# Attention summaries of a fused attention and two-MLP kernel: k, v and phi as head pairs on 128 partitions, in smaller loads

## The chip, the cores and the metric

The kernel runs on one core of a Trainium2 chip. The metric is the device time of one execution in microseconds (us); of three runs the median counts.

## The reference, cut to what matters

There are 8 batches of 8 heads, 576 tokens of 64 numbers, and 32 memory slots. For each head, `phi` is turned into weights over the tokens, which condense k and v to 32 summary rows; the queries then attend to these rows. The result (4608 x 512) goes through two MLPs of width 2048.

```python
a = np.exp(phi - np.max(phi, axis=2, keepdims=True))      # over the tokens
a = a / (np.sum(a, axis=2, keepdims=True) + 1e-09)
k_m = np.einsum('bhsm,bhsd->bhmd', a, k)
v_m = np.einsum('bhsm,bhsd->bhmd', a, v)
scores = scale * np.matmul(q, k_m.transpose(0, 1, 3, 2))
attn = softmax(scores)                                     # over the 32 rows
x = np.matmul(attn, v_m)                                   # heads side by side: 4608 x 512
h = x @ w_in;  x = (h * sigmoid(1.702 * h)) @ w_out        # first MLP
h = x @ w_in2; x = (h * sigmoid(h)) @ w_out2               # second MLP
```

The four weight matrices arrive as 64-bit floats; all else is 32-bit.

## The kernel before, in words

The program has four stages. The first does attention and the first product of the first MLP; the other three do the remaining products with seven block products in place of eight, through intermediate tensors in DRAM (`gs`, `xs`). The change touches only the first stage.

**The slots.** The first stage is a list of 256 slots, 32 to a batch: slot 32*b + 2*f + hf makes 128 of the 2048 columns (f) for one half of the batch's tokens (hf, 288 tokens). `first1` (L314) issues six matmuls of 288 columns on PE (TensorE), a tanh on ACT (ScalarE, L327) and a product on DVE (VectorE, L328) that writes tile `g`. After both halves of an f, `g_store` (L330) stores the 288 KB of `g` to `gs`. There are five `g` buffers and four PSUM buffers for `h`, so PE can run up to four slots ahead of ACT, and ACT at slot 2*(f+5) needs the store of tile f to have landed.

**What a slot multiplies.** The moving operand is `attnT` (the attention weights of a half, `soft_t` to `soft3`, L260 to L298, written as a high and a low part). The stationary one is `slab`: the v summaries times 512 columns of w_in (`wp_mm`, `wp_hi`, `wp_lo`, L300 to L310). A slab (b, c) covers 8 slots. `scores` and `wp_mm` share one PSUM buffer, `aa`, so each waits until the other's reader has emptied it.

**The summaries of a batch.** `load_phi` and `load_kv` (L119, L124) bring 0.59 MB of phi and 2.36 MB of k and v on 96 partitions, six tokens each: one transfer for phi, and k and v each in two transfers of four heads (576 KB). One `kv` buffer holds four heads, so the second group of heads is loaded only after the matmuls of the first. For batches 0 and 1 the second group goes into spare weight buffers, in eight transfers (L130). Then: the maximum over tokens (`fold`, five DVE operations, or one reduction for batch 0, L152), a transpose, a reduction and a broadcast by PE (L157 to L175), subtraction and exponential in two halves (L180, L185), the sum on POOL (GpSimd), 48 matmuls of 96 rows x 32 x 128 columns that give the summaries (`kv_mm`, L189), the division (`kv_norm`, L208), four transposes and a copy (`kvT`).

**w_in.** It comes in 16 pieces of 128 x 512 (four column groups j of four), each converted by two ACT operations (L93, L94), two of DVE (L101, L102) and one of POOL (L104).

**What sets the order.** Each engine executes its own list in order. `at(slot, kind, function)` puts a step into a slot; `plan_attention` (L730) gives the slots for batches 1 to 7 by a table; the code from L800 does so for batch 0, whose steps stand at slots -20 to 0, and for w_in. Up to slot 24 a scheduler reorders what was recorded; from there on the recorded order is final. All transfers are issued by SP (SyncE) on one queue, in order; a transfer whose buffer isn't free yet holds back those behind it.

Of the kernel before, what the change touches and what calls it, by code (L numbers as in the profile page):

```python
# [8 lines left out]
F32 = mybir.dt.float32  # L9
# [12 lines left out]
def attn_moe_moe(ctx: ExitStack, tc: tile.TileContext, q, k, v, phi, w1i, w1o, w2i, w2o, out):  # L22
# [28 lines left out]
    ones = const.tile([128, 1], F32)  # L51
# [67 lines left out]
    def load_phi(b):  # L119
        t = att.tile([P, H, C6, M], F32, tag="phi", name="phi")  # L120
        nc.sync.dma_start(out=t, in_=phi[b].rearrange("h (p c) m -> p h c m", c=C6))
        st["phi", b] = t

    def load_kv(b, g):  # L124
        t = att.tile([P, 2, 4, C6, D], F32, tag="kv", name="kv")
        for i, src in enumerate((k, v)):
            nc.sync.dma_start(out=t[:, i], in_=src[b, 4 * g:4 * g + 4].rearrange("h (p c) d -> p h c d", c=C6))
        st["kv", b, g] = [t[:, :, j] for j in range(4)]

    def load_kv_early(b, rooms):  # L130
# [15 lines left out]
    def fold(b, name, op, eng):  # L146
        x = st["phi", b]
        t = st[name, b] = att.tile([P, H, M], F32, tag=name, name=name)
        for c in range(1, C6):
            eng.tensor_tensor(out=t, in0=t if c > 1 else x[:, :, 0], in1=x[:, :, c], op=op)  # L150

    def phi_fold0(name, op):  # L152
        st[name, 0] = att.tile([P, H, M], F32, tag=name, name=name)
        nc.vector.tensor_reduce(out=st[name, 0], in_=st["phi", 0].rearrange("p h c m -> p h m c"),
                                axis=AX.X, op=op)

    def phi_max_t(b):  # L157
        pm = st.pop(("pm", b)).rearrange("p h m -> p (h m)")
        a = st["a", b] = psa()
        for g in range(2):  # L160
            nc.tensor.transpose(a[:, g * P:(g + 1) * P], pm[:, g * 128:(g + 1) * 128], ident[:P, :P])

    def phi_max_r(b):
        nm = att.tile([128, 2], F32, tag="nm", name="nm")
        nc.vector.tensor_reduce(out=nm, in_=st.pop(("a", b))[:, 0:2 * P].rearrange("p (g s) -> p g s", g=2),
# [3 lines left out]
    def phi_max_b(b):  # L169
        nm = st.pop(("nm", b))  # L170
        a = st["a", b] = psa()
        for g in range(2):
# [906 lines left out]
```

## Time and profile before

| | us |
|---|---|
| median of three runs | 1552.33 (1549.19 to 1562.49) |
| the profiled execution | 1554.82, its span 1553.0 |
| slot 0 starts; from slot 1 on PE runs on | at 42.62; at 57.76 |
| end of the first stage (last of 256 slots) | 424.75 |
| the other three stages | 424.75 to 1553.0 |

The profile gives for each engine when it was busy, and for each idle stretch what ended it (`<-`). The clock is TensorE's granted clock, 1.00 for 2.4 GHz and 0.50 for 1.2 GHz. DMA share is the mean busy share of the 16 transfer engines. A matmul of 32-bit floats appears as two instructions on PE, one in the reduced format `fp32r` (those of L322) as one.

### The profile page before, as it was taken

To read this page: it belongs to the slowest core of one execution; us is meant where nothing else is said; L and a number is where in the kernel's file an instruction comes from. 1 tells how busy PE (TensorE), PEld (TensorE's weight loads), DVE (VectorE), ACT (ScalarE), POOL (GpSimd) and SP (SyncE) were. 2 spreads that over 40 slices of the span, in tenths; PEclk is the share of its full clock that TensorE was granted. 3 is DMA by queue.
4 is the path that set the end of the run, shared out by engine and by line. 5 is a ranking of instruction groups with operands and counts; after the bars stand their busy time and mean duration, and the time that the engine had idled before them with its cause. 6 is when DMAs were issued, how large, how long until landed. Compare 5 with 4: busy or idle time off the path is not lost. (4 is left out here: it accounts for less than half of the span.)

```text
span 1553.0 us, 27494 instructions
## 1 busy us (share of the span) xinstructions
PE 1446.3 (93%) x10432; PEld 1355.6 (87%) x10432; DVE 1158.2 (75%) x1742; ACT 797.8 (51%) x1415; POOL 206.3 (13%) x175
## 2 busy tenths in 40 slices
PE   4789889989879999999989999999998999999998
PEld 2567677778779999999878999999997999999998
DVE  5767666676668878887787877877788777767765
ACT  4545455656534554544545656656565444444443
POOL 2422445441200101010000010110000000000000
PEclk7689899999999999999999999999998999999999
DMA  8677778664737366365334455555456425325230
GB/s 236 195 210 219 203 211 231 219 200 167 248 133 241 98 217 221 102 224 191 104 99 150 153 189 202 165 191 186 169 177 226 144 71 194 112 103 193 86 129 31
DMA packets 202085, 265.54 MB, mean 171 GB/s; under 512 B 51168, under 2 KB 173024, under 8 KB 201952
## 3 DMA queue, kind: packets, MB, share of 16 engines
q1 hardware_dynamic: 201952, 263.77, 52.6%
q8 instruction: 82, 1.34, 0.4%
q14 instruction: 51, 0.42, 0.1%
HBM read 159.91 MB, written 102.76 MB: 169 GB/s over the span
## 5 line engine op out<-in xcount | busy, mean ns | idle before, releaser
L517 PE MATMUL p<-op,wq 128*128 128x384 f32 x2016 | 365.8, 340 | 21.8 <-DVE op L64 12.8
L517 PEld LDWEIGHTS p<-op,wq 128*128 128x128 f32 x2016 | 352.5, 189 | 34.9 <-DVE op L64 23.4
L677 PE MATMUL p<-wq,op 128*128 128x256 f32 x3024 | 360.6, 282 | 4.1 <-DVE gq L619 3.5
L677 PEld LDWEIGHTS p<-wq,op 128*128 128x128 f32 x3024 | 360.2, 191 | 4.8 <-DVE gq L619 4.0
L500 ACT CAST op<-rr 128x768 fp32r<-128x768 f32 x216 | 178.2, 834 | 182.5 <-PE p L677 78.3
L64 DVE TENSOR_TENSOR op<-rr,op 128x768 fp32r<-128x768 f32 x216 | 209.9, 975 | 82.0 <-ACT op L500 79.4
L322 PEld LDWEIGHTS h<-attnT,slab 128*128 128x128 f32 x1536 | 225.2, 203 | 50.9 <-DVE g L328 25.3
L322 PE MATMUL h<-attnT,slab 128*128 128x288 f32 x1536 | 254.2, 318 | 11.6 <-DVE g L328 10.4
L605 PE MATMUL xb<-xq,wq 128*128 128x384 f32 x1152 | 221.5, 341 | 10.8 <-ACT e L637 4.8
L605 PEld LDWEIGHTS xb<-xq,wq 128*128 128x128 f32 x1152 | 202.8, 190 | 16.2 <-ACT e L637 6.0
L328 DVE SCALAR_TENSOR_TENSOR g<-g,h 128x288 f32<-128x288 f32 x256 | 110.2, 444 | 98.9 <-ACT g L327 98.1
L605 PE MATMUL y<-xq,wq 128*128 128x384 f32 x864 | 167.7, 338 | 1.4 <-ACT e L665 0.8
L64 DVE TENSOR_TENSOR op<-r,op 128x768 fp32r<-128x768 f32 x120 | 116.7, 975 | 61.1 <-ACT op L500 60.9
L327 ACT ACTIVATE g<-h 128x288 f32<-128x288 f32 x256 | 103.0, 415 | 106.4 <-PE h L322 66.7
L500 ACT CAST op<-r 128x768 fp32r<-128x768 f32 x120 | 99.7, 834 | 110.8 <-PE p L517 48.7
L605 PEld LDWEIGHTS y<-xq,wq 128*128 128x128 f32 x864 | 152.6, 189 | 2.5 <-ACT e L665 1.5
L614 ACT ACTIVATE gq<-e 128x384 f32<-128x384 f32 x144 | 75.6, 525 | 105.3 <-DVE e L61 102.6
L619 DVE SCALAR_TENSOR_TENSOR gq<-gq,e 128x384 f32<-128x384 f32 x144 | 93.8, 657 | 27.3 <-ACT gq L614 24.6
L104 POOL TENSOR_TENSOR wst<-wst 128x512 int32<-128x512 int32 x24 | 34.1, 1420 | 503.1 <-DVE wst L102 242.7
L428 ACT CAST wq<-wst 128x512 fp32r<-128x512 f32 x83 | 51.2, 618 | 49.4 <-DVE wst L64 24.8
L61 DVE TENSOR_TENSOR e<-e,y 128x384 f32<-128x384 f32 x96 | 52.3, 550 | 17.9 <-PE y L605 15.0
L247 PE MATMUL aa<-w,kvT 64*32 64x512 f32 x512 | 41.1, 673 | 19.7 <-DVE nat L264 15.8
(115 smaller groups left out, 1354.2 us busy)
## 6 DMA issues: line engine op xcount, KB each, us to landing
rr<-gs SPq DMA_DIRECT2D x120, 384.0 KB, 6.2
gs<-g SPq DMA_DIRECT2D x128, 288.0 KB, 4.0
gs<-gq SPq DMA_DIRECT2D x192, 192.0 KB, 2.0
r<-gs SPq DMA_DIRECT2D x72, 384.0 KB, 5.5
xs<-o SPq DMA_DIRECT2D x24, 384.0 KB, 4.4
xr<-xs SPq DMA_DIRECT2D x24, 384.0 KB, 4.5
out_dram<-o SPq DMA_DIRECT2D x24, 384.0 KB, 2.8
q<-in_q_dram SPq DMA_DIRECT2D x124, 72.0 KB, 3.7
```

The costliest lines, as they stand in the source:

```text
L61: eng.tensor_tensor(out=out, in0=a, in1=b, op=ALU.add)
L64: eng.tensor_tensor(out=out, in0=a, in1=b, op=ALU.subtract)
L322: nc.tensor.matmul(out=h, lhsT=slab[b, f // 4, g][:, wi, f0:f0 + 128], rhs=x[:, g, xi], start=(g == 0 and n == 0), stop=(g == 1 and n == 2))
L327: nc.scalar.activation(out=t, in_=h, func=ACTF.Tanh, scale=0.851)
L328: nc.vector.scalar_tensor_tensor(out=t, in0=t, scalar=1.0, in1=h, op0=ALU.add, op1=ALU.mult)
L428: nc.scalar.copy(out=t[:, :, 0], in_=wst[m, c, k])
L500: nc.scalar.copy(out=t[:, :, 0], in_=s)
L517: nc.tensor.matmul(out=out[:, d, :HB], lhsT=w[:, s, wi, d * 128:(d + 1) * 128], rhs=t[:, s, gi], start=(start and p == 0 and s == 0 and n ...
L605: nc.tensor.matmul(out=out, lhsT=w[:, s, wi, f0:f0 + 128], rhs=x[:, s, xi], start=(start and s == 0 and n == 0), stop=(s == 1 and n == 2), ...
L614: nc.scalar.activation(out=t, in_=h, func=ACTF.Tanh)
L619: nc.vector.scalar_tensor_tensor(out=t, in0=t, scalar=1.0, in1=h, op0=ALU.add, op1=ALU.mult)
L677: nc.tensor.matmul(out=out[:, d], lhsT=t[:, u, gi, d * 128:(d + 1) * 128], rhs=w[:, u, wi], start=(start and d != 1 and p == 0 and u == 0 ...
```

## The change

- k, v and phi lie on 128 partitions: a pair of heads, each with 64 partitions of nine tokens. phi comes in four transfers of 144 KB, k and v in eight of 288 KB, all into one `phi` and one `kv` buffer per batch. The transfers of a batch are put into slots two or three apart, in place of one or two slots for all.
- The maximum is one DVE reduction; subtraction and exponential are one operation each; the sum takes eight POOL operations of half the width.
- The summaries take 72 matmuls of 64 rows x 32 x 128 columns; the two heads of a pair write two PSUM buffers. The sums take one matmul with a two-column block matrix instead of two, and two transposes replace four.
- At the start q of the first half stands ahead of w_in; w_in's four column groups have rooms of their own, and groups 1 to 3 are converted and multiplied later: the slabs c = 1, 2, 3 of batch 0 at slots 5, 13, 21 in place of 1, 9, 17. The scores of both halves of batch 0 stand ahead of the first slab.
- Batch 1's steps move later (its second scores from slot 22 to 26, its first slab from 25 to 29), and DVE does both halves' softmax differences there.

```diff
+    def load_phi(b, n):
+        if n == 0:
+            st["phi", b] = att.tile([128, 4, C9, M], F32, tag="phi", name="phi")
+        for j in (2 * n, 2 * n + 1):
+            nc.sync.dma_start(out=st["phi", b][:, j].rearrange("p c m -> p (c m)"),
+                              in_=phi[b, 2 * j:2 * j + 2].rearrange("h (p c) m -> (h p) (c m)", c=C9))
+    def load_kv(b, n):
+        if n == 0:
+            st["kv", b] = att.tile([128, 2, 4, C9, D], F32, tag="kv", name="kv")
+        i, j = divmod(n, 4)
+        nc.sync.dma_start(out=st["kv", b][:, i, j].rearrange("p c d -> p (c d)"),
+                          in_=(k, v)[i][b, 2 * j:2 * j + 2].rearrange("h (p c) d -> (h p) (c d)", c=C9))
...
+    def phi_fold(b, name, op, eng):
         x = st["phi", b]
+        t = st[name, b] = att.tile([128, 4, M], F32, tag=name, name=name)
+        if eng is nc.vector:
+            eng.tensor_reduce(out=t, in_=x.rearrange("p j c m -> p j m c"), axis=AX.X, op=op)
+            return
+        for c in range(1, C9):
             eng.tensor_tensor(out=t, in0=t if c > 1 else x[:, :, 0], in1=x[:, :, c], op=op)
...
-    def kv_mm(b, g):
...
-        for c in range(C6):
+    def kv_mm(b):
+        a = st["kvps", b] = [psa(), psa()]
         e = st["phi", b]
+        x = st.pop(("kv", b))
+        for c in range(C9):
             for j in range(4):
-                nc.tensor.matmul(out=a[32 * j:32 * j + 32, 256 * g:256 * g + 2 * D], lhsT=e[:, 4 * g + j, c, :],
-                                 rhs=kv[j][:, :, c, :], start=(c == 0), stop=(c == C6 - 1))
+                for s in range(2):
+                    r = slice(64 * s, 64 * s + 64)
+                    nc.tensor.matmul(out=a[s][32 * j:32 * j + 32, 0:2 * D], lhsT=e[r, j, c], rhs=x[r, :, j, c],
+                                     start=(c == 0), stop=(c == C9 - 1))
...
+        freed = {2: -18, 3: -32}.get(b, -33)
+        for n in range(2):
+            at(z - 6 if first else z + freed + 2 * n, "d", load_phi, b, n)
+        for n in range(8):
+            at(z - 5 if first else z + freed + 1 + (2 * n if b < 4 else 3 * n), "d", load_kv, b, n)
...
-        for hf, s in enumerate((14, 22) if first else (6, 14)):
+        for hf, s in enumerate((19, 26) if first else (6, 14)):
...
+    W1ROOM = ((0, 1, 2, 3), (4, 5, 6, 7), (8, 9, 10, 11), (12, 13, 14, 14))
+    for n in range(2):
+        load_phi(0, n)
+    for n in range(8):
+        load_kv(0, n)
+    for p in range(4):
+        load_q(0, 0, p)
+    for kk in range(4):
+        w1_load(W1ROOM[0][kk], kk, 0)
...
-    for hf, s in enumerate((-10, -5)):
+    for hf, s in enumerate((-11, -8)):
...
-            s = (-14, -4, 4, 12)[j]
+            s = (-9, 0, 9, 17)[j] + (kk if j else 0)
...
-            plan_wprime(b, c, 32 * b - 7 + 8 * c)
+            plan_wprime(b, c, (-7, 5, 13, 21)[c] if b == 0 else 29 if (b, c) == (1, 0) else 32 * b - 7 + 8 * c)
```

SP's list in a middle batch, the loads of batch 7 (`phi`, `kv`, `q`) among the stores of `g`. Before:

```order
L143 DMA q<-in_q_dram 96x3x64 x2
L121 DMA phi<-in_phi_dram 96x8x192
L127 DMA kv<-in_k_dram 96x4x384
L127 DMA kv<-in_v_dram 96x4x384
L332 DMA gs_7_92<-g 128x576
L143 DMA q<-in_q_dram 96x3x64 x2
L332 DMA gs_7_92<-g 128x576
L332 DMA gs_0_85<-g 128x576
```

The same place in the change (`load_phi` is L123, `load_kv` L130, the stores L312):

```order
L123 DMA phi<-in_phi_dram 128x288 x2
L312 DMA gs_7_92<-g 128x576
L130 DMA kv<-in_k_dram 128x576
L123 DMA phi<-in_phi_dram 128x288 x2
L312 DMA gs_7_92<-g 128x576
L140 DMA q<-in_q_dram 96x3x64 x2
L130 DMA kv<-in_k_dram 128x576
L312 DMA gs_0_85<-g 128x576
L140 DMA q<-in_q_dram 96x3x64 x2
L312 DMA gs_0_85<-g 128x576
L130 DMA kv<-in_k_dram 128x576
```

Three transfers of 1.73 MB in a row became pieces of 144 to 288 KB, with a store of `g` between one and the next.

PE's list at the start: the transposes of q (`a<-ident,q`), the scores of batch 0's halves (`aa<-qT,kvT`), the first slab (`aa<-w_101,kvT`) and the slots (`h`). Before:

```order
L236 MATMUL a<-ident,qe 128x96 x3
L247 MATMUL aa<-qT,kvT 32x288 x2
L247 MATMUL aa<-w_101,kvT 32x512 x8
L236 MATMUL a<-ident,q 128x96 x3
L247 MATMUL aa<-qT,kvT 32x288
L236 MATMUL a<-ident,q 128x96 x6
L247 MATMUL aa<-qT,kvT 32x288 x5
L322 MATMUL h<-attnT,slab 128x288 x6
L236 MATMUL a<-ident,q 128x96 x3
L247 MATMUL aa<-qT,kvT 32x288 x2
L247 MATMUL aa<-w_101,kvT 32x512 x9
L322 MATMUL h<-attnT,slab 128x288 x54
```

In the change:

```order
L216 MATMUL a<-ident,qe 128x96 x3
L227 MATMUL aa<-qT,kvT 32x288 x7
L216 MATMUL a<-ident,q 128x96 x3
L227 MATMUL aa<-qT,kvT 32x288
L216 MATMUL a<-ident,q 128x96 x3
L227 MATMUL aa<-qT,kvT 32x288 x3
L216 MATMUL a<-ident,q 128x96 x3
L227 MATMUL aa<-qT,kvT 32x288 x2
L216 MATMUL a<-ident,q 128x96 x3
L227 MATMUL aa<-qT,kvT 32x288 x2
L227 MATMUL aa<-w_101,kvT 32x512 x8
L302 MATMUL h<-attnT,slab 128x288 x6
```

All eight scores of the second half now precede the first slab; before, they stood behind it and around the first slot's six matmuls.

DVE's list around the low part of the second half's weights (`attnT`), with which slot 1 can start. Before:

```order
L101 TENSOR_SCALAR w_101<-w_101 128x512
L290 STREAM_TRANSPOSE at<-nat 128x576
L102 SCALAR_TENSOR_TENSOR w_101<-raw,w_101 128x512
L101 TENSOR_SCALAR w_101<-w_101 128x512
L64 TENSOR_TENSOR attnT<-at,attnT 128x2x288
L102 SCALAR_TENSOR_TENSOR w_101<-rawe,w_101 128x512
L101 TENSOR_SCALAR w_101<-w_101 128x512 x2
```

In the change:

```order
L270 STREAM_TRANSPOSE at<-nat 128x576
L101 TENSOR_SCALAR w_101<-w_101 128x512
L308 SCALAR_TENSOR_TENSOR g<-g,h 128x288
L102 SCALAR_TENSOR_TENSOR w_101<-rawe,w_101 128x512
L64 TENSOR_TENSOR attnT<-at,attnT 128x2x288
L101 TENSOR_SCALAR w_101<-w_101 128x512 x2
L102 SCALAR_TENSOR_TENSOR w_101<-rawe,w_101 128x512
```

Ahead of that `attnT` row stand 12 of the 16 L102 of w_in before, and 7 in the change; the other 9 stand among the slots.

## Rows read from the trace of the kernel before

**Rows 1.** The page: the span of the profiled execution.

```profile
span 1553.0 us, 27494 instructions
```

**Rows 2.** Busy us (instructions) by stretch: PE, PEld, DVE, ACT, POOL; clock, DMA share, GB/s.

```profile
0.00:57.76 57.76, 31.08 (x210) 15.12 (x210) 40.50 (x61) 29.32 (x52) 16.58 (x18) 0.69 0.92 266
57.76:102.30 44.54, 39.41 (x348) 33.12 (x348) 28.64 (x62) 18.34 (x42) 11.27 (x11) 0.83 0.54 153
102.30:344.00 241.70, 213.66 (x2164) 177.20 (x2165) 166.80 (x363) 137.97 (x320) 108.70 (x99) 0.94 0.73 210
344.00:380.80 36.80, 36.80 (x369) 31.19 (x368) 25.12 (x59) 21.86 (x53) 7.64 (x7) 1.00 0.55 184
380.80:424.75 43.95, 39.53 (x293) 33.68 (x293) 28.24 (x59) 25.91 (x60) 13.38 (x10) 0.92 0.71 229
```

**Rows 3.** Waits in 0 to 425: total us, times, longest us.

```profile
ACT g L327 <- DMA gs<-g: 36.9, 16, 6.0
...
PE aa L247 <- DVE nat L264: 15.8, 8, 4.2
```

**Rows 4.** Timeline of SP's queue, 306 to 320: start, us, instruction, count.

```profile
306.93 0.65 SPq L121 DMA_DIRECT2D phi<-in_phi_dram  x1
307.62 0.53 SPq L127 DMA_DIRECT2D kv<-in_k_dram  x1
308.20 0.95 SPq L127 DMA_DIRECT2D kv<-in_v_dram  x1
309.19 1.31 SPq L332 DMA_DIRECT2D gs<-g  x1
...
318.87 1.32 SPq L332 DMA_DIRECT2D gs<-g  x2
```

**Rows 5.** Timeline of all engines behind these transfers; in brackets the idle time.

```profile
319.67 0.71 ACT L327 ACTIVATE g<-h 128x288 f32<-128x288 f32 x2 [6.02 <-DMA gs<-g]
...
322.53 1.96 PE L247 MATMUL aa<-w,kvT 64*32 64x512 f32 x16 [4.21 <-DVE nat L264]
...
324.42 1.81 PE L322 MATMUL h<-attnT,slab 128*128 128x288 f32 x6
```

**Rows 6.** Timeline of PE in an undisturbed stretch, 278 to 296.

```profile
280.98 0.71 PE L247 MATMUL aa<-qT,kvT 64*32 64x288 f32 x16
281.62 2.65 PE L322 MATMUL h<-attnT,slab 128*128 128x288 f32 x18
284.20 1.09 PE L247 MATMUL aa<-w,kvT 64*32 64x512 f32 x16
285.22 3.44 PE L322 MATMUL h<-attnT,slab 128*128 128x288 f32 x24
288.59 1.52 PE L197 MATMUL a<-kv,phi 96*32 96x128 f32 x48
290.04 3.44 PE L322 MATMUL h<-attnT,slab 128*128 128x288 f32 x24
```

**Rows 7.** DVE busy from the first half's scores to slot 1 (clock, DMA).

```profile
31.20:57.70 26.50, 25.04 (x43) 0.50 0.85 259
```

**Rows 8.** Timeline of DVE at the start: two transposes of scores, last low part.

```profile
31.20 0.85 DVE L264 STREAM_TRANSPOSE nat<-aa 128x288 f32<-128x288 f32 x2 [5.29 <-PE aa L247]
...
46.67 0.85 DVE L264 STREAM_TRANSPOSE nat<-aa 128x288 f32<-128x288 f32 x2 [1.31 <-PE aa L247]
...
55.85 1.85 DVE L64 TENSOR_TENSOR attnT<-at,attnT 128x576 fp32r<-128x576 f32 x1
```

**Rows 9.** Groups by line, 0 to 102: count, busy us, mean ns.

```profile
L102 DVE SCALAR_TENSOR_TENSOR w<-rawe,w 128x512 int32<-128x512 int32 x14 | 12.9, 920 | 0.2
...
L101 DVE TENSOR_SCALAR w<-w 128x512 int32<-128x512 int32 x16 | 8.1, 509 | 0.0
...
L64 DVE TENSOR_TENSOR slab<-aa,slab 128x512 fp32r<-128x512 f32 x8 | 5.2, 666 | 0.3 <-ACT slab L306 0.3
```

**Rows 10.** The page's transfers: count, size, us from issue to landing.

```profile
gs<-gq SPq DMA_DIRECT2D x192, 192.0 KB, 2.0
```

More of the change, by code (lines that the diff above doesn't have):

```diff
@@ L171, in phi_max_b @@
         a = st["a", b] = psa()
-        for g in range(2):
-            nc.tensor.matmul(out=a[:P, g * 128:(g + 1) * 128],
-                             lhsT=nm[:, g:g + 1].to_broadcast([128, P]), rhs=ident,
-                             start=True, stop=True)
-    def half(t, g):
-        return t[:, 4 * g:4 * g + 4]
-    def phi_sub(b, g):
-        t = half(st["phi", b], g)
-        mx = st["a", b][:P, g * 128:(g + 1) * 128].rearrange("p (h o m) -> p h o m", h=4, o=1)
-        nc.vector.tensor_tensor(out=t, in0=t, in1=mx.to_broadcast([P, 4, C6, M]), op=ALU.subtract)
@@ L185, in phi_exp, with phi_sub @@
-    def phi_exp(b, g):
-        t = half(st["phi", b], g)
-        nc.scalar.activation(out=t, in_=t, func=ACTF.Exp)
-    def kv_mm(b, g):
-        if g == 0:
-            st["kvps", b] = psa()
-        a = st["kvps", b]
+        for s in range(2):
+            nc.tensor.matmul(out=a[64 * s:64 * s + 64, 0:128], lhsT=nm[:, s:s + 1].to_broadcast([128, 64]),
+                             rhs=ident, start=True, stop=True)
+    def phi_sub(b):
+        t = st["phi", b]
+        mx = st.pop(("a", b))[:, 0:128].rearrange("p (j o m) -> p j o m", j=4, o=1)
+        nc.vector.tensor_tensor(out=t, in0=t, in1=mx.to_broadcast([128, 4, C9, M]), op=ALU.subtract)
@@ L200, in es_mm @@
     def es_mm(b):
-        a = st["kvps", b]
-        es = st.pop(("es", b)).rearrange("p h m -> p (h m)")
-        for g in range(2):
-            n = 256 * g + 2 * D
-            nc.tensor.matmul(out=a[:, n:n + 2], lhsT=es[:, g * 128:(g + 1) * 128],
-                             rhs=ones[:P].to_broadcast([P, 2]), start=True, stop=True)
+        nc.tensor.matmul(out=st["kvps", b][0][:, 2 * D:2 * D + 2], lhsT=st.pop(("es", b)).rearrange("p j m -> p (j m)"),
+                         rhs=blk, start=True, stop=True)
@@ L745, in plan_attention @@
         at(z + mb, "p", phi_max_b, b)
[L746 to L757 removed]
+        at(z + sb, "e", phi_sub, b)
+        at(z + ex, "e", phi_exp, b)
+        at(z + es, "e", phi_fold, b, "es", ALU.add, nc.gpsimd)
+        at(z + mm, "p", kv_mm, b)
+        at(z + mm + 1, "p", es_mm, b)
         at(z + norm, "e", kv_norm, b)
@@ L787, in attn_moe_moe @@
     make_identity(nc, ident)
-    nc.vector.memset(ones, 1.0)
+    nc.vector.memset(blk, 0.0)
+    for s in range(2):
+        nc.vector.memset(blk[64 * s:64 * s + 64, s:s + 1], 1.0)
     def w1_load(n, kk, j):
-        t = wo_p.tile([128, 512, 2], I32, tag=f"wo{n}", name="rawe") if n < 10 else raw()
+        t = wo_p.tile([128, 512, 2], I32, tag=f"wo{n}", name="rawe") if n < 14 else raw()
         st["w1", kk, j] = wload(w1i, rows(kk), cols(j), t)
```

131 lines of the change are left out of this document (40 added, 91 removed).

## The prediction

> **What bounds the kernel now.** I read the stretches of the first stage first, because the diff touches nothing else. The span is 1553.0 us [rows 1]; the profiled execution took 1554.8, so 1.8 lie around the span, and the median of the runs is 2.5 below that execution. The first stage ends at 424.75 and I leave the 1128 us behind it as they are. In the stretches [rows 2] the reader is to look at PE's busy time and at the clock together. From 344.0 to 380.8 PE has no idle time at clock 1.00: there the stage runs as PE can. From 102.3 to 344.0, five batches, PE is idle for 241.70 - 213.66 = 28.0 us and the clock is 0.94. Up to 57.76 the clock is 0.69 and PE does little; transfers run at 266 GB/s there, a busy share of 0.92.
>
> Who stops PE in the five batches? Among the waits [rows 3] ACT waits 16 times, 36.9 us in all, for a store of g to land, and PE waits 8 times, 15.8 us, for the transpose that empties `aa`. One instance shows that these are one thing. At 306.9 to 309.2 SP issues phi, k and v, 1.73 MB, and the next store of g stands right behind them [rows 4]. At 266 GB/s these 1.73 MB are 6.5 us of transfer. ACT then stands for 6.02 us until a store has landed, with all g buffers full; DVE's transpose comes late behind ACT's tanh; PE stands 4.21 us; and the work after that starts at the lower of the two clock levels, 1.96 us for 16 instructions and 1.81 for six [rows 5] where the undisturbed rows show 1.09 us for the 16 and 3.44 us for 24 matmuls of the slots [rows 6].
>
> What would a batch take without it? The stretch from 344.0 to 380.8 lacks only one group of summary matmuls, 290.04 - 288.59 = 1.45 us [rows 6], and the two small steps on the maximum, which I estimate at 0.6: 36.8 + 1.45 + 0.6 = 38.9 us. The five batches took 241.7 / 5 = 48.3 each. So 47.2 us are lost in all, 28.0 as idle time and 19.2 as slow clock behind it.
>
> **The change part by part.** *Loads in pieces.* The stores now stand among pieces of 144 to 288 KB, so a store has at most about a megabyte ahead of it, not 1.73 MB and more. The bytes remain: 210 GB/s times 241.7 us is 50.8 MB, 10.15 MB a batch, which at the 266 GB/s of the start needs 38.2 us [rows 2]. That is almost exactly PE's 38.9 us. So the stalls can't all go: with both near their limit a store must now and then be late. I let a third of the loss stand, 15.7 us (a batch of 42.0 us, 242 GB/s): -31.5 us. The ends are -47.2, all of it, and 0, rival 1.
>
> *The start.* Before, the first half's scores are ready for DVE at 31.20, the second half's at 46.67, and slot 1 gets its last operand at 57.70 [rows 8]: two chains of 11 us, one behind the other. Now both halves' scores precede the first slab on PE, and DVE's list interleaves the chains. In the 26.50 us from the one end to the other DVE is busy for 25.04 [rows 7], so its list is what counts. Between the same ends the new list lacks six L101, five L102 and two slab differences: 6 x 0.509 + 5 x 0.920 + 2 x 0.666 = 9.0 us [rows 9]. That leaves 17.5 us; for waits on the exponentials, which those instructions used to cover, I add 1.5 (0 to 3): 19.0. The beginning moves too. q comes 0.59 MB earlier against w_in, all four transposes of q stand ahead of the scores instead of alternating with them, and the reduction over 1152 instead of 1536 elements is shorter; against it, the copy of the summaries stands on ACT behind three w_in conversions, whose data now land 0.59 MB / 266 GB/s = 2.2 us later. I take 28.5 for 31.20 (27 to 31.2, no gain). Slot 1 then starts at 28.5 + 19.0 = 47.5 instead of 57.7: -10.2 us (44.5 to 50.2 gives -13.2 to -7.5).
>
> *What is late next.* Nine conversions of w_in, not four, now fall among the first slots: 5 x (0.509 + 0.920) = 7.1 us of DVE [rows 9], and two softmax differences more, about 1.5. DVE was busy for 28.64 of the 44.54 us up to the 25th slot, PE for 39.41 [rows 2]; 37.3 us still fit, so most of it hides beside PE, yet the new list has a block of conversions without a g between, and a slab can't be made before its column group is converted. +2.5 us (0 to 8.6).
>
> *Batch 1.* Its second scores stand at slot 26 for use at slot 33. Seven slots at 3.44 / 4 = 0.86 us are 6.0 us; the chain took 11.0 at the start among other work. +2 us (0 to 5). Behind its DVE steps the g products queue, and PE waits for those.
>
> *The summary matmuls.* 48 became 72 of half the height, so 144 instructions on PE, not 96. The old ones start 1.45 us / 48 = 30.2 ns apart, four column strips side by side [rows 6]. Had the new ones this pace, they would take 4.35 us for 2.90. But the 64x32 tiles of the scores and slabs run eight side by side: 16 instructions take 0.64 us with 288 columns and 1.02 with 512, so 1.70 ns a column, and 0.37 us with 128 [rows 6]. Nine such sixteens are 3.3 us, which I take, being nearest in shape: +0.4 a batch, +3 for eight batches. The ends are 2.1 us a batch (the start paid once, 9 x 128 x 1.70 ns + 0.15) and 4.35: -6 to +12. The smaller work around them (one transpose for two, two for four, a sum matmul less, single operations for halves) only shortens lists that are busy beside PE; I count it at nothing, and if PE's few are not hidden, they are a gain below 1 us a batch.
>
> The Trainium skill, "TensorE: Matmul & The Clock Gate", section "Wait — 56ns, not 53.3ns?", says that matmuls start no closer than about 25 ns however small they are. By that the 144 take at least 3.6 us, the low end is shut, and the term would be +6 instead of +3. No row here has instructions closer than 30 ns, so the trace does not contradict it.
>
> *The pieces' issue.* Twelve transfers instead of five a batch are seven more rows on SP; an issue takes 0.5 to 1 us there [rows 4], 3.5 to 7 us of a 42 us batch on a queue that is not full. Nothing, unless SP waits for a free buffer; the new loads start one slot after the matmuls that free it, as late as the stores around them.
>
> *Sum.* -31.5 - 10.2 + 2.5 + 2 + 3 = -34.2. The profiled execution would take 1554.8 - 34.2 = 1520.6, and the median, 2.5 below, **1518**.
>
> **The rivals.** 1. *The queue stays as full.* The bytes are the same, and 0.73 busy share at 210 GB/s [rows 2] is perhaps all that this mix of 256-byte q rows, stores and loads allows. Then the stores stay late and the batches keep their 48.3 us; the start alone gives -10.2 + 2.5 + 2 + 3 = -2.7: 1550. Against it: 266 GB/s at the start, where q's rows are in the mix, and stalls that stand right behind the large loads [rows 4, 5].
>
> 2. *Each piece costs its own time (slower).* A transfer of 192 KB lands 2.0 us after its issue [rows 10]. If none of that overlapped, seven more transfers would add 14 us to the 38.2 of a batch; 52.2 against 48.3 is +3.9 five times, +19.5, with the start's -2.7: +17, **1569**. The place is the queue in every batch from 1 to 5; it decides from 1.44 us a piece on, (48.3 - 38.2) / 7. Against it: k and v of four heads came in 144 KB transfers at the start and 266 GB/s still flowed [rows 2].
>
> The Trainium skill, "DMA: Bandwidth & Descriptors", section "Bandwidth", advises transfers of 1 MiB or more for 75% of the peak, and its table has 64 KB at 138 GB/s. Taken for single transfers, that is this rival; taken for a queue with several in flight, the 266 GB/s of this trace speak against it.
>
> 3. *The conversions stop the first slots.* All 8.6 us of DVE and the 5 us of batch 1 come on the path: -10.2 + 8.6 + 5 - 31.5 + 3 = -25, 1527. The block of conversions speaks for it, DVE's 16 idle us of 44.5 against it.
>
> That the change doesn't do what it says I leave out: SP's list shows the pieces between the stores.
>
> **How the numbers follow.** My forecast has 0.71; rival 1 0.11, rival 2 0.04, rival 3 0.14. My case's own ends, all terms at once, are -66 and -6; not all fall one way, so I keep -58 for the low end, 1494, and go to **1540** at the top, which takes in rival 3 and a half-kept loss, and leaves most of rival 1 outside. About 1% is what a measurement of this kernel can tell from no change, 1536.8 on the fast side. Forecast and rival 3 lie below that but for about 0.03: faster 0.82. Rival 1 and that rest: same 0.13. Rival 2 and a little: slower 0.05.
>
> **What would show it.** Right: ACT's waits for gs<-g at 12 us or less in all; PE idle time of the five batches at about 10 us and clock at 0.97 or more; a transfer rate near 240 GB/s there; slot 1 going on at 47.5 (44 to 51); summary matmuls at 3.3 us a batch. Wrong in the main step: ACT's waits above 25 us, or moved to SP waiting for kv's buffer. Wrong at the start: the first transpose of scores at 31 or later, or slot 25 not before 100. If the summary matmuls take over 5 us or PE waits for the POOL sum each batch, the terms of PE are wrong.

## The result and the profile after

| | before | after |
|---|---|---|
| median of four runs | 1551.29 us (1549.19 to 1562.49) | 1535.83 us (1533.84 to 1536.92) |
| ratio | | 0.9884, 95% interval 0.9836 to 0.9933 |
| profiled execution | 1554.8 us | 1535.27 us |
| span | 1553.0 us [rows 1] | 1533.2 us |
| end of the first stage | 424.75 us [rows 2] | 406.20 us |
| work behind it | 1128.3 us | 1127.0 us |

The change makes the kernel 1.2% faster by this ratio, 1.0% by the medians; 2.2% was forecast (1518 for 1552.33). The stages behind the first hardly moved, so the difference is to be found inside the first one. The stretches of the kernel after, in the columns of [rows 2], cut where slot 1 begins (49.95) and at the stop that has to be explained:

```profile
0.00:49.95 49.95, 26.68 (x235) 12.33 (x235) 28.67 (x48) 21.94 (x40) 9.20 (x13) 0.70 0.79 245
49.95:67.00 17.05, 16.08 (x108) 12.44 (x106) 14.63 (x25) 12.21 (x26) 6.31 (x6) 0.97 0.85 280
67.00:83.00 16.00, 7.65 (x23) 1.90 (x22) 10.70 (x15) 3.56 (x10) 12.35 (x13) 0.64 0.18 55
83.00:108.83 25.83, 23.06 (x269) 19.04 (x269) 13.93 (x30) 8.00 (x20) 1.01 (x2) 0.83 0.61 190
108.83:152.80 43.97, 40.90 (x481) 32.97 (x479) 33.24 (x68) 22.78 (x54) 12.33 (x15) 0.96 0.74 228
152.80:362.16 209.36, 193.69 (x2322) 159.93 (x2321) 152.30 (x330) 129.97 (x311) 103.78 (x109) 1.00 0.71 225
```

The reader is to see three things. Slot 1 comes earlier: its last operand, the low part of the second half's `attnT`, is ready at 49.77 + 0.76 = 50.53, where it was 57.70 before [rows 8].

```profile
49.77 0.76 DVE L64 TENSOR_TENSOR attnT<-at,attnT 128x576 fp32r<-128x576 f32 x1
```

(49.95 is the first of slot 1's six matmuls, and four of them do without the low part. The 57.76 of the kernel before is the fifth, which waited for it; in the change the fifth starts at 50.99.) The long middle runs at clock 1.00, where before it had 0.94. And from 67 to 83, PE is busy for 7.65 of 16 us, at a clock of 0.64, with the transfers all but standing (55 GB/s): this stop was not there before.

The same batches side by side: from the first slab of batch 1 to the first of batch 6 it was 241.63 us and is now 210.26 (with four slots fewer, since the first slab of batch 1 now stands four slots later):

```profile
114.82:325.08 210.26, 191.51 (x2296) 156.84 (x2295) 155.43 (x329) 128.17 (x306) 104.04 (x108) 1.00 0.77 241
```

Waits of the kernel after in its first 412 us, which answer to [rows 3]:

```profile
ACT g L307 <- DMA gs<-g: 21.5, 8, 9.1
...
PE aa L227 <- DVE nat L244: 6.7, 7, 1.9
```

Of the 21.5 us, 9.1 are one instance behind the stop at 67 us: SP stood 14.8 us, up to 77.84, for a q buffer that PE's transposes at 77.07 set free, and the stores of `g` stand behind that load in its list; inside the five batches it is 9.9 us in six waits, where it was 34.3.

**The stop at 67 us.** PE's timeline in the kernel after:

```profile
65.27 1.88 PE L302 MATMUL h<-attnT,slab 128*128 128x288 f32 x12
67.08 1.04 PE L227 MATMUL aa<-w,kvT 64*32 64x512 f32 x2
70.57 1.21 PE L227 MATMUL aa<-w,kvT 64*32 64x512 f32 x4 [2.46 <-POOL w L104]
72.59 1.92 PE L227 MATMUL aa<-w,kvT 64*32 64x512 f32 x4 [0.80 <-POOL w L104]
75.22 1.92 PE L227 MATMUL aa<-w,kvT 64*32 64x512 f32 x4 [0.71 <-POOL w L104]
...
82.67 0.85 PE L302 MATMUL h<-attnT,slab 128*128 128x288 f32 x2 [4.38 <-DVE g L308]
...
83.93 4.07 PE L185 MATMUL a<-kv,phi 64*32 64x128 f32 x72
...
92.08 2.17 PE L185 MATMUL a<-kv,phi 64*32 64x128 f32 x72
```

The slab c = 2 of batch 0 stands at slot 13, one slot behind the last conversion of its column group (slots 9 to 12). PE has made two of its 16 instructions ahead of time and comes back to it at 67.08. POOL's last three steps of the conversion, L104, end only at 70.5, 72.5 and 75.2; the third is the first of the three in the last row, the other two belong to the fourth column group:

```profile
68.80 1.72 POOL L104 TENSOR_TENSOR w<-w,rawe 128x512 int32<-128x512 int32 x1
...
71.08 1.46 POOL L104 TENSOR_TENSOR w<-w,rawe 128x512 int32<-128x512 int32 x1
...
73.88 3.75 POOL L104 TENSOR_TENSOR w<-w,rawe 128x512 int32<-128x512 int32 x3
```

The slab keeps PE from 67.08 to 77.14, 10.1 us; undisturbed it takes 1.09 [rows 6]. 4.0 us of that are waits for L104. PE has finished the slots 10 to 13 by then, but their tanh stand behind the slab's copy in ACT's list, so ACT stands for 9.59 us beside four full `h` buffers:

```profile
77.24 1.07 ACT L286 CAST slab<-aa 128x512 fp32r<-128x512 f32 x2 [9.59 <-PE aa L227]
...
78.78 1.36 ACT L307 ACTIVATE g<-h 128x288 f32<-128x288 f32 x4
```

The `h` buffers come free with the products of `g` on DVE. There the slab and three steps of the fourth group's conversions stand first, so PE stands another 4.38 us:

```profile
79.55 0.68 DVE L102 SCALAR_TENSOR_TENSOR w<-raw,w 128x512 int32<-128x512 int32 x1
...
80.60 1.65 DVE L102 SCALAR_TENSOR_TENSOR w<-raw,w 128x512 int32<-128x512 int32 x1
82.18 1.54 DVE L308 SCALAR_TENSOR_TENSOR g<-g,h 128x288 f32<-128x288 f32 x4
```

The clock is 0.50 by then: half of batch 1's summary instructions (72) take 4.07 us at 83.93; the other half takes 2.17 at 92.08, at clock 1.00.

**The summary matmuls.** PE in an undisturbed stretch of the kernel after:

```profile
331.08 2.25 PE L185 MATMUL a<-kv,phi 64*32 64x128 f32 x144
333.26 1.05 PE L302 MATMUL h<-attnT,slab 128*128 128x288 f32 x6
```

333.26 - 331.08 = 2.18 us for 144 instructions, that is 15.1 ns from start to start. Before, the two groups of 48 took 2 x 1.45 = 2.90 us [rows 6]. But this is the fastest of all the sets. In the stretch from the first slab of batch 2 to that of batch 7 the five sets take 2.82, 3.14, 5.23, 2.75 and 2.18 us, 16.1 in all. The ten groups of the kernel before took 1.45 each and one 2.21, 15.3 in all. What the slow ones have in them shows in the third:

```profile
247.18 2.15 PE L185 MATMUL a<-kv,phi 64*32 64x128 f32 x131 [0.70 <-ACT qT L220]
250.94 0.44 PE L185 MATMUL a<-kv,phi 64*32 64x128 f32 x11 [1.61 <-issue]
```

After two instructions PE waits for ACT's copy of `qT`: the summaries now take two PSUM buffers `a`, there are two in all, and q's transposes use them too. And there is a gap that the profile puts down to "issue". By groups (149.1 to 380.8 before, with nine of the ten groups; 152.8 to 362.2 after):

```profile
L197 PE MATMUL a<-kv,phi 96*32 96x128 f32 x432 | 14.4, 285 | 0.0
...
L185 PE MATMUL a<-kv,phi 64*32 64x128 f32 x720 | 13.3, 271 | 3.3 <-issue 1.6 <-ACT qT L220 1.6
```

### The profile page after: what moved, and what is told of

Same layout as the page of the kernel before. It is cut to its first block, busy times and chain, and to the rows that moved or that the text cites. A ratio compares the mean times of both kernels' runs of the same rounds, so it can differ in the third digit from the quotient of the medians.

```text
span 1533.2 us, 28236 instructions
## 1 busy us (share of the span) xinstructions
PE 1429.5 (93%) x10776; PEld 1334.3 (87%) x10776; DVE 1150.8 (75%) x1710; ACT 789.1 (51%) x1407; POOL 207.2 (14%) x194
## 5 line engine op out<-in xcount | busy, mean ns | idle before, releaser
L497 PE MATMUL p<-op,wq 128*128 128x384 f32 x2016 | 366.1, 341 | 21.2 <-DVE op L64 12.6
L497 PEld LDWEIGHTS p<-op,wq 128*128 128x128 f32 x2016 | 352.7, 189 | 34.3 <-DVE op L64 23.4
L302 PEld LDWEIGHTS h<-attnT,slab 128*128 128x128 f32 x1536 | 214.0, 193 | 55.7 <-issue 21.8
L302 PE MATMUL h<-attnT,slab 128*128 128x288 f32 x1536 | 245.9, 309 | 17.2 <-DVE g L308 10.6
L104 POOL TENSOR_TENSOR wst<-wst 128x512 int32<-128x512 int32 x24 | 34.1, 1422 | 500.6 <-DVE wst L102 406.9
L227 PE MATMUL aa<-w,kvT 64*32 64x512 f32 x512 | 44.7, 626 | 11.8 <-DVE nat L244 6.7
```

The lines of the kernel that those rows point to most:

```text
L302: nc.tensor.matmul(out=h, lhsT=slab[b, f // 4, g][:, wi, f0:f0 + 128], rhs=x[:, g, xi], start=(g == 0 and n == 0), stop=(g == 1 and n == 2))
L497: nc.tensor.matmul(out=out[:, d, :HB], lhsT=w[:, s, wi, d * 128:(d + 1) * 128], rhs=t[:, s, gi], start=(start and p == 0 and s == 0 and n ...
```

## The experiments

Two questions were open: what ate the gain of the start, and what in the batches made them shorter. Each profiled run is placed by three times on PE's timeline: the first slab of batch 2, the first slab of batch 7, and the end of the last slot. The middle difference, batches 2 to 6, has nothing of the start in it. "Start" is the first of these times, and holds batches 0 and 1. These times are of one execution each. Eight runs have the batches 2 to 6 of the change as they are (the change and the seven runs below it in the table); they lie between 207.9 and 211.8 us, so a difference of less than 4 us there says nothing.

| run | start | batches 2 to 6 | end | median | ratio to before (95%) |
|---|---|---|---|---|---|
| before | 149.12 | 231.71 | 424.9 | 1550 to 1552 | |
| the change | 152.81 | 209.35 | 406.4 | 1535.83 | 0.9884 (0.9836 to 0.9933) |
| es1_dve | 153.17 | 210.63 | 407.5 | 1535.03 | 0.9895 (0.9874 to 0.9916) |
| old_start | 138.89 | 211.12 | 393.8 | 1523.98 | 0.9822 (0.9803 to 0.9840) |
| conv_early | 146.16 | 208.75 | 399.5 | 1530.50 | 0.9881 (0.9858 to 0.9903) |
| old_b1 | 149.98 | 211.42 | 404.6 | 1531.64 | 0.9886 (0.9857 to 0.9916) |
| old_b1_conv | 143.45 | 209.78 | 396.6 | 1529.54 | 0.9873 (0.9851 to 0.9895) |
| scores_early | 150.08 | 207.94 | 400.9 | 1533.43 | 0.9878 (0.9852 to 0.9904) |
| paced | 138.89 | 211.79 | 393.4 | 1524.25 | 0.9819 (0.9791 to 0.9847) |
| together | 156.64 | 237.44 | 438.0 | 1566.05 | 1.0087 (1.0065 to 1.0108) |
| kv_twice | 155.62 | 224.62 | 424.3 | 1556.87 | 1.0043 (1.0023 to 1.0063) |
| large | 157.62 | 214.70 | 415.6 | 1544.73 | 0.9965 (0.9948 to 0.9982) |
| row173 | 152.81 | 217.41 | 414.4 | 1542.52 | 0.9936 (0.9915 to 0.9957) |
| pieces_only | 154.61 | 236.04 | 435.1 | 1558.03 | 1.0037 (1.0016 to 1.0058) |

**The start: es1_dve.** In batch 1, POOL's token sum stands between the conversions. It goes to DVE.

```diff
-        at(z + es, "e", phi_fold, b, "es", ALU.add, nc.gpsimd)
+        at(z + es, "e", phi_fold, b, "es", ALU.add, nc.vector if first else nc.gpsimd)
```

> The changed kernel with one edit: the token sum of batch 1 by DVE in one reduction instead of eight POOL operations. Theory A (the hole from 67 to 89 us is made by these eight operations, which stand on POOL ahead of w_in's conversions and wait for the exponential): the third column group is converted about 8 us earlier, PE's idle 8 us there go, SP's wait for a q buffer (14.8 us) and ACT's wait for a store (9.1 us) shrink with it; 6 to 13 us below the changed kernel, about 1525. Theory B (the hole is the conversions' own DVE and ACT work, whatever POOL does): within 3 us of the changed kernel.

1535.03, no difference, as theory B had it. POOL's sum is not what holds the conversions up: PE's wait for L104 stays, now 4.66 us in one piece, and so does the one for `g` (4.38).

**The start: old_start.** Start and timetable of batch 1 as in the kernel before; new layout and pieces stay.

```diff
-            (0, 3, 5, 7, 9, 10, 11, 13, 15, 17, 18) if first else
+            (-4, -1, 0, 1, 2, 3, 5, 6, 8, 10, 11) if first else
...
-        for hf, s in enumerate((19, 26) if first else (6, 14)):
+        for hf, s in enumerate((14, 22) if first else (6, 14)):
...
-            s = (-9, 0, 9, 17)[j] + (kk if j else 0)
+            s = (-14, -4, 4, 12)[j]
...
-            plan_wprime(b, c, (-7, 5, 13, 21)[c] if b == 0 else 29 if (b, c) == (1, 0) else 32 * b - 7 + 8 * c)
+            plan_wprime(b, c, 32 * b - 7 + 8 * c)
```

> The changed kernel with the start of the kernel before: order of the first loads, slots of batch 0's scores, w_in conversions and slabs, and batch 1's timetable; layout and pieces stay. Theory A (the late conversions cost the start 13 us, its earlier scores gain 8): slot 26 at about 103 us instead of 108.8, so 4 to 8 us below the changed kernel, about 1529. Theory B (the new start is a gain, and the hole comes from the layout's steps): 5 us or more above the changed kernel, 1540 or more.

1523.98, 12 us below the change: theory A in kind, and more than the 4 to 8 us that it named. Its stretches up to slot 1, up to the first slab of batch 1, and one batch more:

```profile
0.00:57.02 57.02, 26.96 (x253) 12.93 (x253) 38.55 (x62) 28.78 (x51) 16.76 (x18) 0.71 0.82 267
57.02:95.94 38.92, 34.91 (x387) 29.55 (x387) 29.98 (x54) 16.77 (x41) 12.29 (x15) 0.90 0.56 175
95.94:138.89 42.95, 39.55 (x470) 32.32 (x469) 31.22 (x65) 23.02 (x55) 12.20 (x15) 1.00 0.80 249
```

Slot 1 gets its last operand 6.4 us later than in the change (56.96 against 50.53), and batch 2 begins 13.9 us earlier. The new start is a loss. It hides a gain of the rest: with the old start, the new layout and pieces bring batch 2 to 138.89, 10.2 us ahead of the kernel before. PE's timeline shows why the same work did no harm there:

```profile
51.80 1.92 PE L227 MATMUL aa<-w,kvT 64*32 64x512 f32 x4 [5.66 <-POOL w L104]
...
57.02 3.25 PE L302 MATMUL h<-attnT,slab 128*128 128x288 f32 x12 [2.31 <-DVE attnT L64]
```

PE waits 5.66 us for a conversion here too, but ahead of slot 1, which has to wait for the second half's weights (`attnT`) until 57.02 anyway.

**The start: conv_early, old_b1, old_b1_conv.** Which part of the new start loses: the place of the conversions, or batch 1's timetable? The first moves the conversions,

```diff
-            s = (-9, 0, 9, 17)[j] + (kk if j else 0)
+            s = (-9, 0, 4, 12)[j] + (kk if j else 0)
```

> The changed kernel with the conversions of w_in's third and fourth column group five slots earlier in the order (slots 4 to 7 and 12 to 15 instead of 9 to 12 and 17 to 20); slabs and the timetable of batch 1 stay. Theory A (the third slab stands in PE's row one slot behind the last of its conversions, so PE waits for them from 67 us on): PE's wait for POOL's L104 goes, slot 26 begins at 97 to 103 instead of 108.8, the time is 6 to 12 us below the changed kernel's 1535. Theory B (the nine conversions' own work on ACT, DVE and POOL among the first slots is too much, wherever it stands): the hole moves to earlier slots, slot 26 at 106 to 111, time within 3 us of 1535.

the second takes batch 1's timetable back, with its scores, q and summaries,

```diff
-            (0, 3, 5, 7, 9, 10, 11, 13, 15, 17, 18) if first else
+            (-4, -1, 0, 1, 2, 3, 5, 6, 8, 10, 11) if first else
...
-        for hf, s in enumerate((19, 26) if first else (6, 14)):
+        for hf, s in enumerate((14, 22) if first else (6, 14)):
```

> The changed kernel with batch 1's timetable as before (summaries from slot -4, scores at slots 14 and 22); the new order of the first loads, of the conversions and of the first scores stays. Theory A (the loss of 11 us among the first slots is that of conversions and the third slab): slot 26 at 106 to 110, time within 4 us of 1535. Theory B (the loss comes from batch 1's steps, packed into slots 0 to 26): slot 26 at 99 to 102, time 6 to 10 us lower.

and the third does both.

> Both edits together: conversions of groups 3 and 4 five slots earlier, and batch 1's timetable as before. Theory A (conversions): as the first of these runs within 3 us. Theory B (batch 1): as the second within 3 us. If both count: the sum of the two gains, near 1520.

Conversions: 6.7 us earlier at batch 2; batch 1's timetable: 2.8; both: 9.4, the sum. In the medians it is 5.3, 4.2 and 6.3 us, and the third run is far from the 1520 that it had for the sum. Theory A of the first run is right in kind and a little below its size. In the second run theory A holds by its own bounds (slot 26 at 106.5, 1531.64 within 4 us of 1535), and its four runs spread from 1527.5 to 1535.9. So that the conversions' place counts is shown; that batch 1's timetable counts rests on single profiled executions. In conv_early PE's wait for L104 falls to a quarter of a microsecond, and the wait for `g` behind the slab stays:

```profile
67.60 1.04 PE L227 MATMUL aa<-w,kvT 64*32 64x512 f32 x2 [0.23 <-POOL w L104]
...
76.27 0.85 PE L302 MATMUL h<-attnT,slab 128*128 128x288 f32 x2 [4.22 <-DVE g L308]
```

With both edits DVE has no idle time left around that place, 17.96 of 18.00 us. That may be why no more came of it; no run takes work off DVE:

```profile
60.00:78.00 18.00, 13.31 (x205) 9.79 (x204) 17.96 (x26) 9.17 (x19) 15.70 (x16) 0.90 0.30 102
```

**The start: scores_early and paced.** Can the early scores be kept, with conversions, slabs and batch 1 as before? On old_b1_conv:

```diff
-            s = (-9, 0, 4, 12)[j] + (kk if j else 0)
+            s = (-9, -4, 4, 12)[j]
...
-            plan_wprime(b, c, (-7, 5, 13, 21)[c] if b == 0 else 29 if (b, c) == (1, 0) else 32 * b - 7 + 8 * c)
+            plan_wprime(b, c, 32 * b - 7 + 8 * c)
```

> The new first loads (q ahead of w_in) and the new place of the first scores, but everything behind them as in the kernel before: conversions of groups 2, 3, 4 at slots -4, 4, 12 in blocks, slabs at -7, 1, 9, 17, batch 1's timetable as before. Theory A (DVE's work, 37 us of it up to slot 25, is only shifted across slot 1: whatever comes later in the order to let slot 1 go on earlier is missing behind it): slot 1 goes on at 53 to 57, time within 3 us of the 1524.0 of the run with the old start. Theory B (early scores are a gain of their own, and only the late conversions and slabs lost it): slot 1 at 50 to 53, 1516 to 1520.

Both theories miss: slot 1 comes early (first matmul at 50.35, last operand at 51.89), as theory B had it, but the time is 1533.43, 9 us above old_start. The slab c = 2 is now at slot 9, and PE meets it before its conversions once more:

```profile
69.75 1.92 PE L227 MATMUL aa<-w,kvT 64*32 64x512 f32 x4 [3.96 <-POOL w L104]
73.45 3.15 PE L227 MATMUL aa<-w,kvT 64*32 64x512 f32 x8 [1.78 <-POOL w L104]
```

PE is at the slab sooner, and the conversions are not earlier but later: the twelfth L104, the last one that this slab needs, ends at 75.9, in old_start at 58.1, in the change at 75.2. In old_start they are done while PE waits for the second half's weights. The opposite edit, on old_start, spreads the conversions of groups 3 and 4 over slots and moves the slabs two slots back:

```diff
-            s = (-14, -4, 4, 12)[j]
+            s = (-14, -4, 4, 12)[j] + (kk if j > 1 else 0)
...
-            plan_wprime(b, c, 32 * b - 7 + 8 * c)
+            plan_wprime(b, c, (-7, 3, 11, 19)[c] if b == 0 else 32 * b - 7 + 8 * c)
```

> The run with the start and batch 1's timetable of before (1524.0), in which the conversions of the third and fourth column group now stand one per slot (slots 4 to 7, 12 to 15) in place of four at once, and the slabs c = 1, 2, 3 of batch 0 at slots 3, 11, 19 in place of 1, 9, 17. Theory A (in the slots 1 to 16 DVE's list of conversions and slabs is what PE waits for, and a block without a g costs a stop of PE): 2 to 6 us lower, 1518 to 1522. Theory B (DVE has too much to do there in any order): within 2 us of 1524.

1524.25, as old_start, theory B. Where slot 1 begins late, spreading the blocks and moving the slabs gave nothing more.

**The batches: together.** All twelve loads of a batch in one place of SP's list.

```diff
-            at(z - 6 if first else z + freed + 2 * n, "d", load_phi, b, n)
+            at(z - 6 if first else z + freed, "d", load_phi, b, n)
...
-            at(z - 5 if first else z + freed + 1 + (2 * n if b < 4 else 3 * n), "d", load_kv, b, n)
+            at(z - 5 if first else z + freed, "d", load_kv, b, n)
```

> The changed kernel with all twelve loads of a batch from 2 on in one slot, in the same pieces. Theory A (the stores of g are late because megabytes stand in a row ahead of them): 2.95 MB in a row are 11 us at 266 GB/s, ACT waits for stores again once a batch, 6 to 10 us; with the slow clock behind it +30 to +60 us, 1565 to 1595. Theory B (128 partitions and longer runs made the gain): within 5 us of the changed kernel.

1566.05, 30 us above the change (theory A), and slower than the kernel before. Its waits in the first 445 us have the shape of [rows 3], larger:

```profile
ACT g L307 <- DMA gs<-g: 50.9, 13, 9.1
...
PE aa L227 <- DVE nat L244: 28.0, 9, 7.7
```

2.9 MB ahead of a store are too much in the new layout as well.

**The batches: kv_twice.** Each of the 72 summary matmuls (144 instructions) of batches 2 to 7 twice; the sums come out doubled.

```diff
-        for c in range(C9):
+        for c in (*range(C9), *range(C9)) if b > 1 else range(C9):
```

> The changed kernel with the 72 summary matmuls of batches 2 to 7 issued twice (the sums come out doubled; the output is not the reference's). One set takes 2.2 us in the profile. Theory A (PE bounds the batches now): +2.2 us six times, +13 (10 to 16). Theory B (transfers at 38 us a batch are the bound, PE has slack): +5 or less.

21 us more, above the 10 to 16 of theory A. The price of a set was too low there, not the kind: on PE's timeline the six doubled sets take 43.1 us, from the first start to the next step, and the six of the change 21.4. So what PE spends more is what the time grows by, and the batches are near what PE can do. One doubled set, 288 instructions, behind its first two:

```profile
162.42 2.60 PE L185 MATMUL a<-kv,phi 64*32 64x128 f32 x166 [0.18 <-ACT qT L220]
166.17 1.96 PE L185 MATMUL a<-kv,phi 64*32 64x128 f32 x120 [1.15 <-issue]
168.06 1.05 PE L302 MATMUL h<-attnT,slab 128*128 128x288 f32 x6
```

**The batches: large and row173.** In batches 2 to 7, the first loads k and v in four transfers of 576 KB instead of eight pieces (a piece of k or v is 288 KB; the expectation names it 144 by mistake, which is a piece of phi):

```diff
+        if b > 1:
+            for i, src in enumerate((k, v)):
+                if n in (0, 4):
+                    j = n // 2
+                    nc.sync.dma_start(out=st["kv", b][:, i, j:j + 2].rearrange("p j c d -> p j (c d)"),
+                                      in_=src[b, 2 * j:2 * j + 4].rearrange("(j s) (p c) d -> (s p) j (c d)", s=2, c=C9))
+            return
```

> The changed kernel with k and v of batches 2 to 7 in two pairs of 576 KB transfers (four heads each, k and v back to back, where the first and the fifth piece stood) in place of eight pieces of 144 KB apart; phi as in the change. Theory A (what counts is how many bytes stand in one row ahead of a store: 1.15 MB at 266 GB/s is 4.3 us, and the whole batch at once cost 30 us): time 0 to 10 us above the changed kernel's 1535, ACT's waits for stores 22 to 32 us. Theory B (the size of a transfer counts by itself, large ones move better): time at or below 1533, and waits no longer than the changed kernel's 21.5 us.

The second also puts phi into the place of the first pair: 1.73 MB in one row, as in [rows 4], with the new layout. (It is three times 576 KB; in the unit in which phi is 0.59 MB, 1.77.)

```diff
-            at(z - 6 if first else z + freed + 2 * n, "d", load_phi, b, n)
+            at(z - 6 if first else z + freed + 1, "d", load_phi, b, n)
```

> As the run with k and v of batches 2 to 7 in transfers of 576 KB, and phi of these batches stands in the same place as the first pair of them: 1.73 MB in one row ahead of the next store, as in the kernel before, with the new layout. Theory A (that row of 1.73 MB is what delayed the stores): the batches 2 to 6, 214.7 us with phi apart and 231.7 in the kernel before, go to 224 to 230 us; the time is 10 to 14 us above the 1544.7 of the run with phi apart, 1554 to 1559; ACT's waits for stores above 32 us. Theory B (the new layout's shorter work for PE and the smaller rest made most of the 22 us that the batches gained): batches within 3 us of 214.7, time within 3 us of 1544.7.

large: 1544.73, 9 us above the change, theory A. row173: 1542.52, not above large: theory B. Its batches take 217.4 us, 8 more than with the pieces and 14.3 fewer than before. Yet most of ACT's waits for stores came back; what did not come back is PE's wait. From the first slab of batch 2 to that of batch 7, before:

```profile
ACT g L327 <- DMA gs<-g: 31.5, 13, 6.0
...
PE aa L247 <- DVE nat L264: 13.3, 4, 4.2
```

and in row173:

```profile
ACT g L314 <- DMA gs<-g: 24.2, 8, 4.7
...
PE aa L234 <- DVE nat L251: 6.0, 6, 1.9
```

In the change these are 9.9 and 5.9 us.

**The batches: pieces_only.** The kernel before, with the loads for batches 3 to 7 in ten pieces of 288 KB.

```diff
-        load({2: -24, 3: -31}.get(b, -34), load_phi, b)
+            for n in range(2):
+                load((-31 if b == 3 else -34) + 2 * n, load_phi, b, n)
...
-        load({2: -28, 3: -31}.get(b, -34), load_kv, b, 0)
+            for n in range(4):
+                load((-30 if b == 3 else -33) + 2 * n, load_kv_piece, b, 0, n)
...
-            load(mm[0], load_kv, b, 1)
+            for n in range(4):
+                load(mm[0] + 2 * n, load_kv_piece, b, 1, n)
```

> The kernel before, with its old layout, start and timetable; only the loads of phi, k and v for the batches 3 to 7 come in pieces: phi in two transfers of 288 KB, k and v in eight of 288 KB, each in a slot of its own, two slots apart, so that a store stands between any two. They fall among the slots of the batches 2 to 6, which take 231.7 us in the kernel before, 217.4 with the new layout and 1.73 MB in one row, 209.4 with both. Theory A (layout and pieces each give their own part, 14 and 8 us): batches 2 to 6 at 222 to 226 us, time near 1543. Theory B (either one is enough to take most of the stalls away): 212 to 217 us, time near 1534. Theory C (with the old layout the transfers themselves take too long, pieces don't help): 229 us or more, within 3 us of the kernel before.

1558.03, slower by 8 us (the profiled execution, 1564.16, is among its slowest): theory C comes nearest, and has the wrong reason. (The loads fall among the batches 1 to 5, not 2 to 6.) The stores are free now, and PE stands for v instead (waits from the first slab of batch 2 to that of batch 7):

```profile
PE a L207 <- DMA kv<-in_v_dram: 16.4, 4, 7.3
...
ACT g L337 <- DMA gs<-g: 2.8, 1, 2.8
```

```profile
168.24 2.77 PE L207 MATMUL a<-kv,phi 96*32 96x128 f32 x44 [7.12 <-DMA kv<-in_v_dram]
```

In the old layout both halves of k and v share one buffer. The second half can be asked for only at slot -11, when the first is used up, and is needed at slot -2. Four pieces, two slots apart, end too late. The new `kv` buffer holds all eight heads, so that the pieces have the whole batch. (Large buffer and layout were not tried apart.)

## Why the prediction was right and wrong

The direction and the size of the main term were right, and 1535.83 lies within 1494 to 1540, near its upper end. Half of the expected gain was lost at one step. Of the signs that the prediction named, three came: clock 1.00 in the five batches, 241 GB/s there, slot 1 between 44 and 51. Three did not: ACT's waits for stores are 21.5 us in all (12 or less), PE's idle time in the five batches is 210.26 - 191.51 = 18.8 us (about 10), and the summary matmuls are not at 3.3 us but between 2.2 and 5.3. And one sign of being wrong at the start came: slot 25 not before 100 (it began at 107.3).

Forecast and measurement of the profiled executions, part by part; because the first slab of batch 1 stands four slots later in the change, 4 x 0.86 = 3.4 us are moved between the second and third row. The first row ends with slot 1's last operand:

| part | forecast | measured |
|---|---|---|
| up to slot 1 | -10.2 | 50.53 - 57.70 = -7.2 |
| slot 1 to the first slab of batch 1 | +2.5 + 2 | 64.29 - 44.64 - 3.4 = +16.2 |
| five batches from there, their summary matmuls with them | -31.5 + 1.9 | 210.26 - 241.63 + 3.4 = -27.9 |
| batches 6 and 7, and what stands behind | +1.1 | +0.3 - 1.0 = -0.7 |
| sum | -34.2 | -19.6 |

**The start: right in kind, short in size.** DVE's list was the thing to count, and the first scores came to it at 29.3 (28.5 forecast). From there to the last operand it took 50.53 - 29.32 = 21.2 us where 19.0 were forecast, so that 50.53 lies just above the range of 44.5 to 50.2.

**"What is late next": the step that failed.** It set +2.5 (0 to 8.6) against nine conversions, because DVE had 37.3 of 44.5 us to do, and +2 (0 to 5) against batch 1. It added up an engine's time over a stretch and did not ask at which slot PE's own list needs the result. The prediction had the clue in one sentence, that a slab can't be made before its group is converted, and then let the idle time pay. In fact the slab stands one slot behind its last conversion on an engine that works in order, so everything behind it waits: a slab of 10.1 us in place of 1.09, of which 4.0 are waits for L104, then 4.4 for `g`, and the lower clock after it. Measured are +16.2 us for the +4.5. Rival 3 named this mechanism, but its price of 8.6 + 5 was still too small. The three runs that take the parts back show it: conversions 6.7 us, batch 1's timetable 2.8, together 9.4 of the 13.9 us that old_start is ahead at batch 2 (6.3 of 11.9 in the medians). The rest is not settled by a run of its own; scores_early points to the same conflict at another slab.

**The batches: the size right, the reason only in part.** The forecast was 42.0 us a batch and 0.4 for the summary matmuls; measured, with the four slots put back, it is (210.26 + 3.4) / 5 = 42.7, and 241 GB/s (242 forecast). Rivals 1 and 2 fall with that. But the prediction gave the whole -31.5 to the pieces. The runs give them 8.0 us of the 22.4 that batches 2 to 6 gained (row173 against the change, single executions) and the rest of the change, with the same 1.73 MB in a row, 14.3. In row173 ACT waits 24.2 us for stores, 9.9 with the pieces and 31.5 before, and PE's wait for the transpose is less than half of what it was: a late store need not stop PE, which is where the prediction took two things for one. That the sum came out is so far luck. What the 14.3 us are (transfers that land sooner, below; the loads' place two slots later against the scores; the steps of a batch at later slots; fewer and shorter operations on PE and DVE) was not separated. The summary matmuls are not among them: 16.1 us for 15.3.

**The summary matmuls: the size by luck.** Forecast were 3.3 us a batch for 2.9; the five sets take 3.2 on the mean. But undisturbed a set takes 2.18, at the low end of 2.1 that the working gave: it took nine groups of 16 and paid for each the 0.15 us by which 16 instructions exceed 128 x 1.70 ns, which in a row of 144 is paid once. What brings the mean up, the waits for the second PSUM buffer and the gaps put down to "issue", the prediction put at nothing. By the Trainium skill, "TensorE: Matmul & The Clock Gate", section "Wait — 56ns, not 53.3ns?", start-to-start never drops below about 25 ns, 3.6 us for the 144. The rows here show 15.1 ns, so for 64x32 tiles, eight side by side, the measurement decides against it.

**The pieces' issue: right.** No loss to the added transfers shows. The Trainium skill, "DMA: Bandwidth & Descriptors", section "Bandwidth", advises transfers of 1 MiB or more. No run here has them, and a step that way was a loss: k and v in transfers of 576 KB, two in a row (large), are 9 us slower than in pieces of 288 KB with stores between them.

A version that beats both kernels is old_start, 1523.98 us, 0.9822 of the time before (0.9803 to 0.9840): the new layout and pieces, with the old start.

## What to carry to other kernels

When work moves behind the point where the main loop starts, look up for each result the slot in which the bounding engine's own list needs it, and what its last producer still has ahead of it; idle time summed over a stretch does not pay for one late operand in an in-order list. Here the earlier start was worth nothing, because the next operand came no earlier. And before loads are cut into pieces, see that the buffer lets them be asked for early enough: pieces without the larger buffer only turned a wait for stores into a wait for data.

## What the runs showed of the hardware that was not expected

Transfers of the same size landed sooner with the new layout. From 150 to 345 us the 576 KB of k and of v took, from issue to landing (median), before:

```profile
kv<-in_k_dram SPq DMA_DIRECT2D x8, 576.0 KB, 7.4
kv<-in_v_dram SPq DMA_DIRECT2D x8, 576.0 KB, 8.6
```

and in row173, where half of them stand in the same row of 1.73 MB, as before:

```profile
kv<-in_k_dram SPq DMA_DIRECT2D x8, 576.0 KB, 5.4
kv<-in_v_dram SPq DMA_DIRECT2D x8, 576.0 KB, 7.1
```

In large, with phi apart, they took 6.2 and 7.4. A row of a partition is 9 x 64 x 4 = 2304 bytes in place of 6 x 64 x 4 = 1536 and there are 128 partitions in place of 96; which of the two counts was not tried, nor what the rest of the queue does to it.

Short matmuls on tiles go at a pace by group of tiles, not by instruction. At clock 1.00, 48 instructions on 96x32 tiles, four side by side, took 1.45 us before (12 groups, 0.12 each). 144 on 64x32 tiles, eight side by side, took 2.18 in the change (18 groups, 0.12). Batch 1's two rows of 72 there, whose records start in groups of four, took 94.18 - 92.08 = 2.10 at clock 1.00 (18 groups, 0.12) and 87.93 - 83.93 = 4.00 at 0.50 (0.22). So two heads of a pair side by side cost no more than one.

Long rows of short matmuls have gaps of more than a microsecond that the profile puts down to "issue": seven in the doubled sets of kv_twice, two in the sets of the change. In kv_twice each of the seven ends 2.2 to 3.2 us after the start of a 16 KB transfer of the queue that the profile calls "instruction" (163.7 for the gap that ends at 166.17). This speaks for the loading of PE's instructions; no run tests it.
